# Stages two and three of a five-stage attention and MLP kernel in one written order, with weight units cut into eight steps

## The chip, the cores and the metric

The kernel runs on one core of a Trainium2 chip. The metric is the device time of one execution in microseconds (us). The engines are TensorE (PE, matmuls; PEld is its weight load), VectorE (DVE), ScalarE (ACT), GpSimd (POOL) and SyncE (SP), which here issues nearly all DMAs.

## The reference, cut to what matters

```python
# attention in chunks of 64, 8 batches x 8 heads x 576 tokens, head size 64
scores = matmul(q_c, k_c.T) / 8;  attn = softmax(scores);  x = matmul(attn, v_c)   # 4608 tokens x 512
# first MLP, 512 -> 1536 -> 512
xn = x / sqrt(mean(x * x) + 1e-6) * rms_g
x = (silu(xn @ w_gate) * (xn @ w_val)) @ w_out
# second MLP, 512 -> 2048 -> 512
h = x @ w_in
out = (h * cos(h)) @ w_out2
```

The weights arrive as 64-bit floats. The kernel takes them apart by integer operations into fp32, splits every fp32 operand into a high and a low half, and multiplies with three matmuls for one (high by high, high by low, low by high).

## The kernel before, in words

**Stages.** Stage one is the attention, the norm, and the first four of the twelve 128-wide column blocks of gate and value as plain products. Stage two is the other eight blocks of gate and value, as two-by-two block products in the seven-product scheme of Strassen and Winograd. Stage three is `w_out` of the first MLP, stage four `w_in` of the second, stage five its `w_out`, all in the seven-product scheme. Stages two to five walk the 4608 tokens in six passes of 768 (NB = 6, halves of H = 384). A *product* below is one of the seven for one group of weights: 12 matmuls of 128x128 by 128x384. Stage two has 4 groups and so 28 products a pass, stage three 3 groups and 21, stages four and five 28 each.

**Stage two (L671 to L780).** Per group the products go 1, then 4 and 3 of the group before, then 2, 6, 5, 7. Products 1, 6, 7 and 4 accumulate in one PSUM bank (`b1`, two of them in turn); after 1, 6 and 7 ACT copies the bank away (`savedg`, L713) before the next of them may write it. DVE adds the copies to banks `b2` and `b5` (L720), and ACT (Silu, L725) or DVE (the multiplication with value, L730) ends a block, which SP stores to `hd`. The operands of the next pass (`operandg`: DVE additions, an ACT cast for the high half, a DVE subtraction for the low) are made one after each product of a pass's last group.

**Weight units.** 44 units (`todo_w`) prepare the weights of stages three to five beside the matmuls. A unit is four raw loads of 128 KB, an ACT pass (L116), four DVE conversions (L119 to L125), for the 16 units of kind "in" an ACT scaling (L232), four DVE sums (L192), two ACT casts (L200), two POOL subtractions (L204) and the stores of the seven results to DRAM (`w_keep`, L213). `w_tick` runs a whole unit after every fourth product of stage two; the last 8 units (LATER) run in stage three, two in each of passes 1 to 4. Stage one prepares the 16 units of stage two in the same way, in the steps a, b, c, d, h, o, k of `prep_step`.

**Stage three (L835 to L914).** `operand2` makes operands five products ahead of PE. A group's next pass comes back from DRAM as one 1.5 MB load (`fetch2`, L303), issued once the last operand of that group is made. The third group of the first pass has its own pool, opened where stage two's tiles lay.

**What sets the order.** Stage one stands in a written table (`ORDER`) that fixes all five queues. Stages two and three are written as loops, and the framework's scheduler orders their instructions on each queue; all queues run in order.

Of the kernel before, what the change touches and what calls it, by code (L numbers as in the profile page):

```python
# [38 lines left out]
LATER = 8  # L39
# [31 lines left out]
SECOND = (1, 2, 6, 7, 5, 4, 3)  # L71
# [8 lines left out]
def kernel(  # L80
# [47 lines left out]
    second_w = [("out1", g, PLACE_A[j]) for j in PRODUCTS for g in range(N1 // 4)]  # L128
    wanted += second_w[:3] + [("h", 0, g) for g in range(N1 // 4)]
    wanted += [("op2", g, k) for g in range(2) for k in range(2)] + second_w[3:]  # L130
    wanted += [("prep", 0, k) for k in range(6)]
# [10 lines left out]
    def free(*tags):  # L142
        for tag in tags:
# [6 lines left out]
            if kind in ("h", "x2"):  # L150
                early[key] = wp.tile([P, 2, H], F32, tag=tag, name="a")
                if kind == "h":
                    a = hd[0][:, k, 0:2, :H]
# [12 lines left out]
    raws, least = [], [LATER]  # L166
# [21 lines left out]
    def w_sums(t, s):  # L188
        ops = ((t[:, 3, :], t[:, 2, :], ALU.add), (s[:, 0, :], t[:, 0, :], ALU.subtract))
        ops += ((t[:, 0, :], t[:, 3, :], ALU.subtract), (t[:, 1, :], s[:, 1, :], ALU.subtract))  # L190
        for n, (a, b, op) in enumerate(ops):
            nc.vector.tensor_tensor(s[:, n, :], a, b, op=op)  # L192

    def w_parts(to, t, s):
        to = [to[0][:, :, 0:3], to[0][:, :, 3:7]] if len(to) == 1 else to
        return zip(to, (t[:, :3, :], s))

    def w_hi(to, t, s):
        for o, a in w_parts(to, t, s):
            nc.scalar.copy(o[:, 0], a)  # L200

    def w_lo(to, t, s):
        for o, a in w_parts(to, t, s):
            nc.gpsimd.tensor_tensor(o[:, 1], a, f32(o[:, 0]), op=ALU.subtract)  # L204

    def w_keep(kind, i, half, to):
# [3 lines left out]
        cut = (slice(0, 7),) if len(to) == 1 else (slice(0, 3), slice(3, 7))  # L210
# [4 lines left out]
    def w_load(get):  # L215
        while len(todo_w) > least[0] and len(raws) < 2:
            raw = get("raw", [P, 4, P], U64)
            raws.append((*todo_w.pop(0), raw))
            w_raw(*raws[-1])

    def w_tick(get):
        if not raws:
            return
        kind, i, half, raw = raws.pop(0)
        t = get("pt", [P, 4, P], U32)
        raw, flat = raw.rearrange("p a b -> p (a b)"), t.rearrange("p a b -> p (a b)")
        convert0(raw, flat)
        convert1(flat)
        convert2(raw, flat)
        t = f32(t)  # L230
        if kind == "in":
            nc.scalar.activation(t, t, AF.Copy, scale=-INV2PI)  # L232
        s = get("ps", [P, 4, P], F32)
        w_sums(t, s)
        to = get("pout", [P, 2, 7, P], F32R)
        to = to if isinstance(to, list) else [to]
        w_hi(to, t, s)
        w_lo(to, t, s)
        w_keep(kind, i, half, to)
        w_load(get)  # L240


    def blocks(raw):

        i = (slice(0, 2), slice(2, 4)), (slice(0, H), slice(H, T))
        return {(r, c): raw[:, i[0][r], i[1][c]] for r in range(2) for c in range(2)}
# [45 lines left out]
    def fetch2(s, g):  # L292
        if s < NB:
            t = rw[g].tile([P, 4, T], F32, tag=f"raw{g}", name="rawh")
            raw[s, g] = blocks(t)
            c = s * T % PIECE
            a = hd[s * T // PIECE][:, g, :, c : c + T]
            if ("h", s, g) in early:
                raw[s, g][0, 0] = early["h", s, g]
                nc.sync.dma_start(out=t[:, :, H:], in_=a[:, :, H:])  # L300
                nc.sync.dma_start(out=t[:, 2:, :H], in_=a[:, 2:, :H])
            else:
                nc.sync.dma_start(out=t, in_=a)  # L303
# [11 lines left out]
    def fetchg(s):  # L315
        if s < NB:
            o = s * T % PIECE
            for r in range(2):
                for c in range(2):
                    rawg[s, r, c] = t = gr.tile([P, 2, H], F32, tag=f"r{r}{c}", name="q")  # L320
                    a = xd[s * T // PIECE][:, 2 * r : 2 * r + 2, o + c * H : o + (c + 1) * H]
                    nc.sync.dma_start(out=t, in_=a)

    def operandg(s, j):
        b = {(r, c): rawg[s, r, c] for r in range(2) for c in range(2)}
        if j == 6:
            nc.vector.tensor_tensor(b[0, 0], b[0, 0], b[0, 1], op=ALU.subtract)
            nc.vector.tensor_tensor(b[0, 0], b[1, 1], b[0, 0], op=ALU.add)
        elif j == 7:
            nc.vector.tensor_tensor(b[0, 1], b[1, 1], b[0, 1], op=ALU.subtract)  # L330
        elif j == 5:
            nc.vector.tensor_tensor(b[0, 1], b[1, 1], b[0, 0], op=ALU.subtract)
        elif j == 4:
            nc.vector.tensor_tensor(b[1, 0], b[1, 0], b[0, 0], op=ALU.subtract)
        a = b[{1: (0, 0), 2: (1, 0), 6: (0, 0), 7: (0, 1), 5: (0, 1), 4: (1, 0), 3: (1, 1)}[j]]
# [868 lines left out]
```

## Time and profile before

| | |
|---|---|
| median of 3 runs | 1701.04 us (1699.08 to 1701.77) |
| the profiled execution | 1701.35 us, its span 1699.6 us |
| PE, DVE, ACT, POOL busy | 96%, 82%, 57%, 11% of the span |
| mean granted TensorE clock | 0.99 |
| DMA | 343 MB, 202 GB/s over the span |

Matmuls overlap in the pipeline, so a busy PE is not yet a PE at its pace. What a stage loses is read from its length against that of a stage of the same matmuls that waits for nothing; what it loses it to is read from the waits of PE, and from there back along the queue that PE waited for.

### The profile page before, as it was taken

How to read it: one execution, taken by the hardware profiler on the slowest of the kernel's cores; microseconds unless marked ns; L12 is line 12 of the kernel's file. 1: busy time of each engine (PE TensorE's matmuls, PEld its weight loads, DVE VectorE, ACT ScalarE, POOL GpSimd, SP SyncE). 2: the span in 40 equal slices, each digit the busy share in tenths (PEclk: the TensorE clock that was granted, in tenths of full speed). 3: DMA queues.
4: the chain of work that ended last, by engine and by line, in shares of the span. 5: the costliest groups of instructions: out<-in, count | busy, mean ns of one | idle time of the engine just before them, and what ended most of it. 6: DMA issues, size and time to landing. Idle time of an engine off the chain costs nothing.

```text
span 1699.6 us, 29170 instructions
## 1 busy us (share of the span) xinstructions
PE 1631.2 (96%) x11208; PEld 1566.0 (92%) x11208; DVE 1385.6 (82%) x1926; ACT 965.4 (57%) x1382; POOL 190.2 (11%) x208
## 2 busy tenths in 40 slices
PE   6999999999999999899999999999999999999999
PEld 5887788889889889899999999999999999999998
DVE  7998886578888888489988768889889978878876
ACT  5777665344555554245554458888888744444433
POOL 2322322022232222001110000000000000000000
PEclk9999999999999999989999999999999999999999
DMA  9588897968768788955556874344334673365341
GB/s 341 180 250 271 267 279 241 387 196 266 214 202 253 218 226 241 369 180 184 181 172 234 271 277 140 112 149 140 130 121 142 204 244 111 87 185 145 115 113 38
DMA packets 338956, 342.98 MB, mean 202 GB/s; under 512 B 87680, under 2 KB 303744, under 8 KB 338816
## 3 DMA queue, kind: packets, MB, share of 16 engines
q1 hardware_dynamic: 338016, 341.02, 62.8%
q8 instruction: 88, 1.44, 0.4%
q14 instruction: 52, 0.43, 0.1%
q10 hardware_dynamic: 800, 0.10, 0.0%
HBM read 197.92 MB, written 143.13 MB: 201 GB/s over the span
## 4 chain that ended last, share of the span: by engine, by line
PE 66%; DVE 17%; DMA 7%; ACT 4%; issue 3%; SPq 1%; POOL 1%; DVEq 0%; ACTq 0%; POOLq 0%
PE b L285 56%; PE v L285 4%; PE g L285 4%; DMA rawh<-hd 3%; DMA raw<-in_w_dram 2%; DVE z L720 2%; DVE ps L192 1%; DVE xt L346 1%; DVE pt L125 1%; DVE z L730 1%; DVE pt L124 1%; DMA hd<-z 1%; PE pt L435 1%; ACT xo L272 1%; DVE xo L273 1%
## 5 line engine op out<-in xcount | busy, mean ns | idle before, releaser
L285 PE MATMUL b<-xo,w 128*128 128x384 f32 x3528 | 622.4, 337 | 15.0 <-ACT xo L272 12.6
L285 PEld LDWEIGHTS b<-xo,w 128*128 128x128 f32 x3528 | 615.4, 189 | 21.7 <-ACT xo L272 16.6
L285 PE MATMUL b<-xt,w 128*128 128x384 f32 x1728 | 316.0, 339 | 23.4 <-ACT z L713 18.4
L285 PEld LDWEIGHTS b<-xt,w 128*128 128x128 f32 x1728 | 302.0, 190 | 33.8 <-ACT z L713 25.0
L285 PE MATMUL b<-x,w 128*128 128x384 f32 x1440 | 264.3, 336 | 1.7 <-DVE z L720 1.6
L285 PEld LDWEIGHTS b<-x,w 128*128 128x128 f32 x1440 | 251.1, 188 | 4.8 <-DVE z L720 3.1
L272 ACT CAST xo<-q 128x768 fp32r<-128x768 f32 x144 | 118.2, 836 | 117.3 <-PE b L285 98.5
L273 DVE TENSOR_TENSOR xo<-q,xo 128x768 fp32r<-128x768 f32 x144 | 135.1, 954 | 53.3 <-ACT xo L272 53.0
L285 PE MATMUL b<-q,w 128*128 128x384 f32 x864 | 158.2, 334 | 0.0
L285 PEld LDWEIGHTS b<-q,w 128*128 128x128 f32 x864 | 150.5, 188 | 0.0
L272 ACT CAST xo<-rawh 128x768 fp32r<-128x768 f32 x102 | 81.7, 834 | 96.5 <-DMA rawh<-hd 51.6
L273 DVE TENSOR_TENSOR xo<-rawh,xo 128x768 fp32r<-128x768 f32 x102 | 92.9, 953 | 25.4 <-ACT xo L272 25.1
L285 PE MATMUL g<-xt,w 128*128 128x512 f32 (+1 forms) x528 | 111.4, 363 | 1.7 <-DVE xt L502 1.7
L285 PE MATMUL v<-xt,w 128*128 128x512 f32 (+1 forms) x528 | 108.7, 357 | 0.3 <-ACT sg L548 0.3
L285 PEld LDWEIGHTS g<-xt,w 128*128 128x128 f32 x528 | 88.2, 194 | 15.8 <-DVE xt L502 2.2
L204 POOL TENSOR_TENSOR pout<-pt,pout 128x384 fp32r<-128x384 f32 x44 | 49.5, 1125 | 474.4 <-ACT pout L200 420.3
L285 PEld LDWEIGHTS v<-xt,w 128*128 128x128 f32 x528 | 85.6, 189 | 13.9 <-ACT sg L548 0.5
L720 DVE TENSOR_TENSOR z<-b,z 128x768 f32<-128x768 f32 x72 | 68.3, 950 | 30.4 <-PE b L285 12.8
L998 DVE TENSOR_TENSOR u<-b,z 128x768 f32<-128x768 f32 x72 | 68.6, 952 | 17.7 <-ACT z L993 16.7
L1014 ACT ACTIVATE q<-q 128x768 f32<-128x768 f32 x72 | 60.8, 844 | 34.8 <-DVE q L1013 34.8
L1016 DVE SCALAR_TENSOR_TENSOR q<-q,u 128x768 f32<-128x768 f32 x72 | 68.6, 952 | 12.7 <-ACT q L1015 12.2
L1013 DVE SCALAR_TENSOR_TENSOR q<-q,u 128x768 f32<-128x768 int32 x72 | 68.6, 953 | 12.4 <-ACT q L1012 12.3
(132 smaller groups left out, 2052.0 us busy)
## 6 DMA issues: line engine op xcount, KB each, us to landing
gd<-q SPq DMA_DIRECT2D x80, 384.0 KB, 2.5
q<-gd SPq DMA_DIRECT2D x80, 384.0 KB, 4.2
w<-kout SPq DMA_DIRECT2D x49, 512.0 KB, 7.4
rawh<-hd SPq DMA_DIRECT2D x15, 1536.0 KB, 7.3
raw<-in_w_dram SPq DMA_DIRECT2D x176, 128.0 KB, 3.2
qk<-in_qk_dram SPq DMA_DIRECT2D x36, 512.0 KB, 5.4
kout<-pout SPq DMA_DIRECT2D x40, 448.0 KB, 3.7
kgv<-wout SPq DMA_DIRECT2D x32, 448.0 KB, 5.6
```

Of the source, the lines that this page charges most:

```text
L124: nc.vector.scalar_tensor_tensor(t, hi, 0xC0000000, t, op0=ALU.bitwise_and, op1=ALU.bitwise_or)
L125: nc.vector.scalar_tensor_tensor(t, lo, 29, t, op0=ALU.logical_shift_right, op1=ALU.bitwise_or)
L192: nc.vector.tensor_tensor(s[:, n, :], a, b, op=op)
L204: nc.gpsimd.tensor_tensor(o[:, 1], a, f32(o[:, 0]), op=ALU.subtract)
L272: nc.scalar.copy(hi, a)
L273: nc.vector.tensor_tensor(lo, a, f32(hi), op=ALU.subtract)
L285: nc.tensor.matmul(acc, a, b, start=first and k == 0 and q == 0, stop=k == n - 1 and q == 2, skip_group_check=True)
L720: nc.vector.tensor_tensor(part, acc, part, op=ALU.add)
L998: nc.vector.tensor_tensor(t, acc, part, op=ALU.add)
L1013: nc.vector.scalar_tensor_tensor(q, k, -1.0, u, op0=ALU.mult, op1=ALU.add)
L1014: nc.scalar.activation(q, q, AF.Sin, scale=math.pi)
L1016: nc.vector.scalar_tensor_tensor(q, q, -PI2, u, op0=ALU.add, op1=ALU.mult)
```

## The change

One table, `ORDER2`, now writes out the order of stages two and three for all five queues. Its tokens are single steps: M is a product of stage two, N one of stage three, A, B, C the PSUM copies, a, e, y the sums, ends and stores, q, h, l additions, high and low of an operand of stage two, u, i, o the same of stage three, G the load of one block, P a step of a weight unit, W, F, J, K, L, V the places that come free for a weight or a block that is waiting to be loaded.

- A weight unit has the steps l (loads), a, b, c, s (scaling, kind "in"), d (sums), g and h (casts), o and p (POOL), k and m (stores), each with its own place. The sums are written into the raw tile, the conversion tile has two buffers, the results two tiles of 3 and 4.
- LATER is 10: units 34 to 43 run in stage three, in passes 1 to 5.
- Stage three's rows of hidden values come back as four blocks of 384 KB each, each loaded when that block is free. Six blocks of its first pass are loaded early into places of their own (before: three), among them all four of the third group. Its first products go 1, 1, 2, 2, 7, 7 over the first two groups before the third group is touched (before: 1, 1, then 1 of the third).
- Stage two's products go 1, 4 and 3 of the group before, 6, 2, 7, 5, and its operands follow.
- The kept weights have high and low side by side (`[P, 7, 2, 2, 2, P]` with the high/low index last but one), so a store writes runs of 1024 B where it wrote 512 B; the matmuls index them accordingly.
- In stage one the table `ORDER` is another one as well (995 tokens for 1009). The sums of its 16 units move from DVE to POOL, it starts on the plain products with column block 2 in place of 0, converts the first weight unit later, and leaves 14 of the 28 weight loads of stage two to `ORDER2`.

```diff
-LATER = 8
+LATER = 10
-SECOND = (1, 2, 6, 7, 5, 4, 3)
+SECOND = (1, 6, 2, 7, 5, 4, 3)
...
+    w1st = [(g, j) for j in (1, 2, 7) for g in range(2)] + [(2, 1), (2, 7)] + [(g, 6) for g in range(3)] + [(2, 2)]
+    w1st += [(g, j) for j in (5, 4, 3) for g in range(N1 // 4)]
+    second_w = [("out1", g, PLACE_A[j]) for g, j in w1st]
...
-        for h in range(2):
-            for o, k in zip(to, cut):
-                nc.sync.dma_start(out=kept[kind, g][:, k, e, h, half], in_=f32(o[:, h]))
+        nc.sync.dma_start(out=kept[kind, g][:, k0 : k0 + to.shape[1], e, half], in_=f32(to))
...
+    def w_step(kind, u):
+        key = todo_w[u]
+        late = u >= len(todo_w) - LATER
...
+        s = f32(raw)[:, : 4 * P].rearrange("p (a b) -> p a b", b=P)
+        if kind == "a":
+            convert0(raw, flat)
+        elif kind == "b":
+            convert1(flat)
+        elif kind == "c":
+            convert2(raw, flat)
         elif kind == "s":
             nc.scalar.activation(t, t, AF.Copy, scale=-INV2PI)
+        elif kind == "d":
+            w_sums(t, s, nc.vector)
...
-                nc.sync.dma_start(out=t, in_=a)
+    def fetch2(s, g, b):
+        raw[s, g, b] = t = rw[g].tile([P, 2, H], F32, tag=f"r{g}{b}", name="rawh")
+        r, c = b // 2, b % 2
+        o = s * T % PIECE + c * H
+        nc.sync.dma_start(out=t, in_=hd[s * T // PIECE][:, g, 2 * r : 2 * r + 2, o : o + H])
...
                 b["s"] = pp.tile([P, 4, P], F32, tag="ps", name="wsum")
-                w_sums(t, b["s"])
+                w_sums(t, b["s"], nc.gpsimd)
...
-            if count[0] % 4 == 0:
-                if count[0] == 4:
-                    w_load(getg)
-                elif pg:
-                    w_tick(getg)
...
+    ORDER2 = """
+        Pl0 M001 q06 q07 h06 l06 A00 h07 l07 q05 M002 M006 q04 h03 B00 M007 h05 l05 M005 M011 l03 h04 l04 C00 Pa0 Pb0
...
+    with tc.manual_schedule(engines=FIXED):
+        for name in ORDER2.split():
+            if name[0] == "P":
+                w_step(name[1], int(name[2:]))
```

What this does to the queues, at three places. First ACT, in a late group of a pass of stage two. The names: `z<-b` is the copy of the PSUM bank that PE waits for, `pout` (after: `wout`) the casts of a weight unit, `pt` (after: `wt`) its first pass and its scaling, `xt` and `x` operand casts. Before:

```order
L713 COPY z<-b_6058 128x768
L232 ACTIVATE pt<-pt 128x512
L200 CAST pout<-pt 128x384
L200 CAST pout<-ps 128x512
L116 ACTIVATE pt<-raw 128x512
L232 ACTIVATE pt<-pt 128x512
L200 CAST pout<-pt 128x384
L725 ACTIVATE z<-z 128x768
L200 CAST pout<-ps 128x512
L713 COPY z<-b_6058 128x768
```

After:

```order
L749 COPY z<-b_5706 128x768
L246 CAST wout<-wraw 128x4x128
L235 ACTIVATE wt<-wt 128x512
L349 CAST x_4560<-q 128x768
L349 CAST xt<-q 128x768
L749 COPY z<-b_5706 128x768
L246 CAST wout<-wt 128x3x128
L246 CAST wout<-wraw 128x4x128
L349 CAST xt<-q 128x768
L116 ACTIVATE wt<-wraw 128x512
L749 COPY z<-b_5706 128x768
```

Before, eight instructions of two weight units and one Silu stood between the first and the second copy of a bank; now the steps of a unit are spread, and four stand between two copies.

Second PE, at the start of stage three. `b1`, `b2` and `b3` are the banks of products 1, 2 and 7, each operand is an `xo`, and `xo_8147` (before) and `xo_8184` (after) are the first of the third group. Before, from the last matmul of the second group's product 1:

```order
L285 MATMUL b1_8160<-xo_8092,w_7647 128x384
L285 MATMUL b1_8160<-xo_8147,w_7663 128x384
L285 MATMUL b3_8214<-xo_8152,w_7823 128x384
L285 MATMUL b1_8160<-xo_8147,w_7663 128x384 x11
L285 MATMUL b3_8214<-xo_8152,w_7823 128x384 x11
L285 MATMUL b3_8214<-xo_8157,w_7837 128x384 x12
```

After:

```order
L290 MATMUL b1_8103<-xo_7755,w_7668 128x384
L290 MATMUL b2_8133<-xo_8101,w_7777 128x384 x12
L290 MATMUL b2_8133<-xo_8146,w_7779 128x384 x12
L290 MATMUL b3_8164<-xo_8148,w_7885 128x384 x12
L290 MATMUL b3_8164<-xo_8181,w_7887 128x384 x12
L290 MATMUL b1_8103<-xo_8184,w_7988 128x384 x12
```

Four products of the first two groups now stand ahead of the third group's first.

Third SP, between two passes of stage three. `rawh<-hd` reads hidden values back, `x2d<-x` stores a result, `raw` (after: `wraw`) and `kout` are the loads and stores of weight units. Before:

```order
L186 DMA raw<-in_w_dram 128x4x32 x4
L906 DMA x2d_72<-x_8752 128x2x384
L303 DMA rawh<-hd_70 128x4x768
L906 DMA x2d_72<-x_8806 128x2x384
L303 DMA rawh<-hd_70 128x4x768 x2
L906 DMA x2d_72<-x_8885 128x2x384
L213 DMA kout_8647<-pout 128x3x128
```

After:

```order
L301 DMA rawh<-hd_70 128x2x384 x2
L841 DMA x2d_72<-x_8684 128x2x384
L301 DMA rawh<-hd_70 128x2x384 x2
L201 DMA kout_7837<-wout 128x3x256
L189 DMA wraw<-in_w_dram 128x4x32 x4
L841 DMA x2d_72<-x_8785 128x2x384
L301 DMA rawh<-hd_70 128x2x384 x6
```

Before, three large loads followed the last operands; now twelve small ones are spread over the end of a pass and the start of the next.

## Rows read from the trace of the kernel before

**Rows 1.** Windows by stage, us: length, busy (instructions) per engine, clock, DMA share, GB/s.

```profile
0.00:319.10 319.10, 294.13 (x3648) 248.96 (x3648) 260.00 (x507) 201.50 (x366) 81.82 (x122) 0.98 0.83 269
319.10:707.30 388.20, 363.95 (x2016) 352.56 (x2017) 305.15 (x469) 191.60 (x283) 87.70 (x70) 0.99 0.80 248
707.30:992.90 285.60, 271.53 (x1514) 266.14 (x1514) 239.49 (x291) 131.71 (x174) 20.69 (x16) 0.98 0.66 217
992.90:1343.60 350.70, 350.70 (x2018) 349.05 (x2017) 300.28 (x350) 290.46 (x376) 0.00 (x0) 1.00 0.41 142
1343.60:1699.60 356.00, 350.91 (x2018) 349.27 (x2016) 280.67 (x311) 150.17 (x186) 0.00 (x0) 1.00 0.47 138
```

**Rows 2.** Waits of PE in stage two: us in total, times, longest.

```profile
PE b L285 <- ACT z L713: 18.4, 16, 3.3
PE b L285 <- DVE z L720: 5.3, 9, 1.1
```

**Rows 3.** Timeline around one of them: start, length, engine, [idle before].

```profile
489.82 1.12 DVE L192 TENSOR_TENSOR ps<-pt,ps 128x128 f32<-128x128 f32 x1
490.97 0.62 ACT L200 CAST pout<-ps 128x512 fp32r<-128x512 f32 x1 [0.51 <-DVE ps L192]
491.50 0.79 ACT L713 COPY z<-b 128x768 f32<-128x768 f32 x1
...
492.34 3.88 PE L285 MATMUL b<-xt,w 128*128 128x384 f32 x13 [3.32 <-ACT z L713]
```

**Rows 4.** Windows of 10 us with a lower granted clock, columns as in rows 1.

```profile
720.00:730.00 10.00, 5.46 (x16) 5.06 (x17) 7.83 (x11) 4.77 (x7) 0.00 (x0) 0.53 0.53 124
490.00:500.00 10.00, 7.66 (x36) 7.66 (x37) 6.19 (x12) 5.86 (x10) 2.18 (x3) 0.83 0.73 210
```

**Rows 5.** Groups of DVE in stage two: busy us, mean ns | idle before.

```profile
L720 DVE TENSOR_TENSOR z<-b,z 128x768 f32<-128x768 f32 x71 | 67.4, 950 | 29.2 <-ACT z L713 12.5 <-PE b L285 11.7 <-DMA w<-kout 5.1
...
L119 DVE TENSOR_SCALAR pt<-pt 128x512 f32<-128x512 f32 x35 | 23.7, 676 | 32.3 <-ACT pt L116 32.3
...
L192 DVE TENSOR_TENSOR ps<-pt,ps 128x128 f32<-128x128 f32 x35 | 19.1, 546 | 0.7
...
L120 DVE TENSOR_SCALAR pt<-pt 128x512 uint32<-128x512 uint32 x35 | 14.8, 424 | 0.9
...
L332 DVE TENSOR_TENSOR q<-q 128x768 f32<-128x768 f32 x6 | 9.3, 1546 | 0.1
```

**Rows 6.** Landing of the weight loads of stage two, DMA view: KB each, median us.

```profile
w<-kgv SPq DMA_DIRECT2D x28, 512.0 KB, 8.5
```

**Rows 7.** Waits in stage three, of PE and of ACT.

```profile
PE b L285 <- ACT xo L272: 12.6, 9, 6.5
...
ACT xo L272 <- DMA rawh<-hd: 51.6, 15, 5.6
```

**Rows 8.** Pieces of PE in stage three, timeline.

```profile
724.50 45.17 PE L285 MATMUL b<-xo,w 128*128 128x384 f32 x241 [6.46 <-ACT xo L272]
...
773.16 0.44 PE L285 MATMUL b<-xo,w 128*128 128x384 f32 x1 [0.42 <-ACT xo L272]
...
819.63 0.45 PE L285 MATMUL b<-xo,w 128*128 128x384 f32 x1 [1.51 <-ACT xo L272]
...
915.18 0.44 PE L285 MATMUL b<-xo,w 128*128 128x384 f32 x1 [1.51 <-ACT xo L272]
```

**Rows 9.** Windows of the start of stage one, columns as in rows 1.

```profile
0.00:40.00 40.00, 24.45 (x458) 20.54 (x461) 31.11 (x60) 20.09 (x38) 9.17 (x20) 0.91 0.99 341
40.00:140.00 100.00, 94.84 (x1385) 85.46 (x1378) 94.99 (x189) 74.06 (x138) 29.70 (x42) 1.00 0.72 223
```

**Rows 10.** Groups of stage one's weight units, columns as in rows 5.

```profile
L204 POOL TENSOR_TENSOR wout<-wsum,wout 128x512 fp32r<-128x512 f32 x16 | 22.0, 1374 | 0.0
...
L204 POOL TENSOR_TENSOR wout<-wt,wout 128x384 fp32r<-128x384 f32 x16 | 16.8, 1052 | 44.3 <-ACT wout L200 33.8 <-DVE z L426 6.2 <-DVE wt L120 3.7
...
L192 DVE TENSOR_TENSOR wsum<-wt 128x128 f32<-128x128 f32 x32 | 9.1, 284 | 0.1
```

More of the change, by code (lines that the diff above doesn't have):

```diff
@@ L191, in w_sums, with w_keep @@
         for n, (a, b, op) in enumerate(ops):
[L192 to L206, printed above, removed]
+            eng.tensor_tensor(s[:, n, :], a, b, op=op)
+    def w_keep(kind, i, half, to, k0):
         g, e = i // 2, i % 2
@@ L290, with block2, blocks2 @@
     raw, ops = {}, {}
[L292 to L302, printed above, removed]
-                nc.sync.dma_start(out=t, in_=a)
+    def fetch2(s, g, b):
[3 more added lines that the diff above has]
+        nc.sync.dma_start(out=t, in_=hd[s * T // PIECE][:, g, 2 * r : 2 * r + 2, o : o + H])
+    def block2(s, g, b):
+        return early["h", g, b] if s == 0 and ("h", g, b) in early else raw[s, g, b]
+    def blocks2(s, g):
+        have = [k for k in range(4) if (s, g, k) in raw or (s == 0 and ("h", g, k) in early)]
+        return {k: block2(s, g, k) for k in have}
     xstack = ExitStack()
@@ L781 @@
-    xstack.close()
     third = ExitStack()
@@ new lines, in storeg, with open2, turn2 @@
+    def storeg(s, g, k):
+        r, c = k // 2, k % 2
+        t0 = s * T + c * H
+        o = t0 % PIECE
+        to = hd[t0 // PIECE][:, g // 2 + 1, 2 * r : 2 * r + 2, o : o + H]
+        nc.sync.dma_start(out=to, in_=sums[s, g, k])
+    def open2():
+        first.close()
+        rw[0] = rw[1] = second.enter_context(tc.tile_pool(name="rw", bufs=1, side="right", reuse_waits="tile"))
+    def turn2():
+        mid.close()
+        xstack.close()
+        pool["xo"] = rest.enter_context(tc.tile_pool(name="xo", bufs=7, reuse_waits="tile"))
+        pool["tp"] = rest.enter_context(tc.tile_pool(name="tp2", bufs=1, reuse_waits="tile"))
+        pool["ps"] = rest.enter_context(tc.tile_pool(name="ps_c", bufs=1, space=PSUM, reuse_waits="tile"))
+        rw[2] = second.enter_context(tc.tile_pool(name="rw3", bufs=1, side="right", reuse_waits="tile"))
@@ new lines, in hi2, with lo2 @@
+    def hi2(s, g, j):
+        if ("op2", g, 0) in place_of and s == 0 and j == 1:
+            to = [wp.tile([P, 2, H], F32R, tag=place_of["op2", g, e], name="xo") for e in range(2)]
+        else:
+            o = pool["xo"].tile([P, 2, 2, H], F32R, tag="xo", name="xo")
+            to = o[:, 0], o[:, 1]
+        nc.scalar.copy(to[0], source2(s, g, j))
+        ops[s, g, j] = to
+    def lo2(s, g, j):
+        to = ops[s, g, j]
+        nc.vector.tensor_tensor(to[1], source2(s, g, j), f32(to[0]), op=ALU.subtract)
@@ new lines, in multiply2 @@
+    def multiply2(s, g, j):
+        bank = BANK[j]
+        opens = j in (1, 2, 7, 4)
+        if opens and g == 0:
+            tag = "b2" if bank == "b4" else bank
+            z[s, bank] = pool["ps"].tile([P, 2, D], F32, tag=tag, name=bank, bufs=2 if bank == "b1" else 1)[:, :, :H]
+        w, x = weight["out1", g, PLACE_A[j]], ops.pop((s, g, j))
+        for p in range(2):
+            steps = [(w[:, e, p, 0], w[:, e, p, 1], x[0][:, e], x[1][:, e]) for e in range(2)]
+            mm3(z[s, bank][:, p], steps, opens and g == 0)
@@ L917 @@
+    rest.close()
     G4 = N2 // 4
```

537 lines of the change are left out of this document (265 added, 272 removed).

## The prediction

> **What bounds the kernel now.** I read the windows by stage first, then the waits of PE in the two stages that the table rewrites, then the timeline back from a long wait, then stage one. In the windows by stage [rows 1] stage four is the yardstick: its 2016 matmuls (6 passes, 28 products of 12) take 350.7 us at a granted clock of 1.00 with PE busy throughout, so 0.174 us for a matmul and 2.09 us for a product. Stage two holds the same 2016 matmuls of the same shape and takes 388.2 us: 37.5 us too many. Stage three holds 1512, worth 263.0 us, and takes 285.6: 22.6 too many. Stage five's 356.0 us hold the same matmuls, the end of the output included, and nothing in the change reaches it. So the two rewritten stages can give back 60 us at most, and PE is the bound: DVE is busy for 305.2 us in stage two and 239.5 in stage three, which fits into 350.7 and 263.0.
>
> In stage two PE waits 23.7 us in 25 pieces [rows 2], and 18.4 of them wait for ACT's copy of a PSUM bank. The timeline shows what that is [rows 3]: the copy itself takes 0.8 us, but it stood behind a weight unit's second cast, which waited for the unit's last sum on DVE, and PE stood for 3.32 us. The rest of the 37.5, some 14 us, is what follows such a wait: in the ten microseconds around it the granted clock is 0.83, a mixture of 2.4 and 1.2 GHz [rows 4].
>
> Stage three loses its 22.6 us at two kinds of place [rows 8]. From its start at 707.3 to 773.16 stand 26 products, worth 54.3 us; they took 65.9, so 11.6 are lost, of which 6.46 are the wait for the third group's first operand, and in the window behind it the clock is 0.53 [rows 4]. After that a pass should take 21 products, 43.8 us: 773.16 to 819.63 is 46.5, and the two up to 915.18 take 95.6, so 2.6 and 7.9 are lost. At those borders ACT's casts wait for the 1.5 MB loads, 51.6 us in 15 waits [rows 7], most of it hidden.
>
> **The change part by part.** *Stage two's order.* It removes no PE work. One unit fewer runs here (34 against 35 between the stage's limits), so DVE's load stays near 305 us, or 0.87 of 350.7. The chance lies in the places: between two copies of a bank stand four ACT instructions instead of eight, and the casts that wait for sums no longer come as a block ahead of the copy. The changed sequence 1, 4, 3, 6, 2, 7, 5 gives the copies of product 1, 6 and 7 two, one and two products of time (4.2, 2.1, 4.2 us) where it was three, one and one; a copy of 0.8 us behind one other ACT instruction of the same size fits into each. So nearly all of the 23.7 us of waits can go, and with them the slow clock. What is late next: first, the opening, where product 6 follows 1 and 2 directly and its operand needs two additions, a cast and a subtraction, some 3.5 us against 2.1 (1 to 2 us). Second, 14 of the 28 weight loads now stand in this stage's SP queue, some directly ahead of the product that reads them in the table (fourth group, first pass); a load lands in 8.5 us [rows 6], and SP reaches the first of them only after stores that wait for POOL, so I count 2 us and bound it by 0 and one full landing, 8.5. Third, the table gives the second and the fourth pass about 8% more of DVE's work than the mean, 55 us and more of 58.5; small hold-ups remain there, 3 us. Fourth, 2 us for waits of single semaphores. That leaves 8 to 9 us of the 37.5: **29 us saved**, between 15 (half the waits come back elsewhere) and 35.
>
> *Stage three's blocks.* The third group's four blocks come early into places of their own and four products of the other groups, 8.4 us, stand ahead of it, against a wait of 6.46: the 11.6 us of the start shrink to about 2. The single blocks are loaded as each comes free, most of them during the last two products of a pass instead of after its last operand; that is up to six multiplications, 12.5 us, earlier for the first two of the four. Of the 10.5 us at the borders I leave 3. The cost: 72 loads instead of 18, hidden on SP, which idles between the passes, and two weight units more. Those lie in pass 5, which had none, so each of passes 1 to 5 holds two as passes 1 to 4 did. A unit's eight DVE instructions at 0.3 to 0.7 us [rows 5] are some 3.5 us, so of the 239.5 us [rows 1] the 8 units are 28, a pass without them 35, and with two 42, for 43.8. That is close, so 1 us more. Stage three then loses 6 of its 22.6: **16.6 us saved**, between 5 and 20.
>
> *Stage one.* DVE is busy 126 of the first 140 us [rows 9] and PE's clock and busy share are low in the first 40, so DVE sets the pace there. The 64 sums leave DVE: 64 times 0.284 is 18.2 us. On POOL the trace has no such sum; the two POOL sizes of a unit, 1.374 us for 512 columns and 1.052 for 384, differ by 0.32 for 128 columns and leave a base of 0.09, so I take 0.41 us, 26 us in all beside POOL's 82 of 319. What POOL does slows some of DVE's work: in stage two the last sum of a unit took 0.546 where it takes 0.284, the first conversion 0.676 against 0.424 of its neighbour, and the operand addition of the row 1.546 against 0.95 of a plain sum [rows 5, 10]. Over 35 units that is some 9 us (35 times 0.26) and 9 (35 times 0.25), and for some 20 such additions 12: 30 us over POOL's 87.7 [rows 1], or 0.34 us for one of POOL's. So the 26 us cost DVE 9, and 9 remain as gain, a third of it in the stretch that DVE bounds. The new table also brings the first normed operands up about 4 us of DVE work earlier, by moving the first unit's conversion back. **6 us saved**, between a loss of 8 (the rule below) and a gain of 14.
>
> The Trainium skill speaks against this part: "SBUF — State Buffer", section "SBUF: two separate sides", has GpSimd and a DVE instruction with two SBUF inputs take the shared ports by an exclusive lock, the other blocked for the whole instruction. The rows above show a third of that as a mean. By the rule the 26 us of POOL would cost DVE 26 and the 6 us gained become some 8 lost; that is the second rival.
>
> *The wider runs of the kept weights and the moved raw buffers* are costed at nothing: DMA is at 0.80 of its time in stage two, and no wait in rows 2 and 7 is for a store. If that cover is gone, the weight loads are what comes late, and it is in the first rival. *Stages four and five* keep their time; the loads of the first weights of stage four start about nine products, 19 us, before it, against a landing of 8.5 each and several together, so 0 to 3 us, taken as 0.
>
> Sum: 29 + 16.6 + 6 = 51.6 us. The profiled execution took 1701.35 us (span 1699.6, 1.75 around it), 0.3 above the median. 1701.35 - 51.6 = 1649.8, and I say **1649 us**.
>
> **The rivals.** *First, the waits move to the SP queue.* One strict order for all queues means that a store that waits for POOL holds every load behind it; then weights and blocks arrive late in each pass. Against it: SP's order was fixed before too, and DMA has a fifth of its time free. If half of stage two's waits come back (15 saved) and half of stage three's (11 saved), with nothing from stage one: 1675 us. *Second, POOL's sums lock DVE in full.* Stage one then loses 8 instead of gaining 6, and DVE sets its pace there: 1649 + 14 = 1663. For it, DVE at 126 of 140 us; against it, the third measured in stage two. *Third, slower.* Every unit now crosses between ACT, DVE and POOL at eight written places, and a place that comes too early holds a queue. The longest single wait of PE is now 3.3 us [rows 2]. If each of the 44 units costs PE 2.7 us, that is 119 us against the 60 lost today: 1699.6 + 1.75 + 59 = 1760. It decides from 1.4 us of PE time for each unit on; today it is 60 / 44, the same 1.4, so the table would have to be no better than the scheduler's order. Between the two copies in the order I see the reverse. *Fourth, no difference:* the written order ends up with the scheduler's waits, 1700.
>
> **How the numbers follow.** Forecast 0.73, first rival 0.11, second 0.07, third 0.06, fourth 0.03. For the range I take both ends of the terms, not all at once: 35 + 20 + 11 saved gives 1635; 15 + 11 + 0 gives 1675, the first rival, whose better half is in. So 1634 to 1674, which leaves out the third and fourth, half of the first, and a little of the forecast's own spread. A measurement of this kernel tells some 0.2% (3.4 us) from no change. Faster: 0.73 + 0.11 + 0.07 = 0.91; the same 0.03; slower 0.06.
>
> **What would show it.** In the changed profile stage two should last about 359 us with PE's waits for the PSUM copy under 5 us and the clock at 1.00 in all but one or two windows; stage three about 269, with no wait over 2 us at its start and none for a block; stage one about 313, with POOL's busy time 26 us up and DVE's some 10 us down. A stage two above 370 says that waits moved: if PE waits for a weight load, it is the first rival, if for ACT behind POOL or DVE, the third. A stage one above 319 is the second. The forecast is wrong if stages two and three together stay above 650 us.

## The result, and the profile after

The changed kernel takes **1651.24 us** (median; 1651.09 to 1651.34) against 1701.4 us beside it: a ratio of 0.9707, interval 0.9691 to 0.9724. The prediction was 1649. The profiled execution took 1651.34 us, its span 1649.1. The sum came out, but not all of its terms did.

The windows by stage answer [rows 1]. Columns: window and length, then busy us (instructions) of PE, weight loads, DVE, ACT and POOL, the granted clock, DMA share, GB/s. The third window ends after the first product of stage four; the fourth is a hole that was not there before.

```profile
0.00:311.10 311.10, 288.79 (x3649) 246.46 (x3649) 239.88 (x434) 199.96 (x361) 112.04 (x184) 0.99 0.83 273
311.10:663.80 352.70, 351.46 (x2017) 349.17 (x2018) 303.42 (x461) 187.74 (x280) 90.86 (x68) 1.00 0.80 259
663.80:929.90 266.10, 264.46 (x1525) 263.94 (x1523) 246.28 (x306) 134.87 (x181) 31.04 (x20) 1.00 0.74 244
929.90:942.90 13.00, 0.17 (x2) 0.05 (x1) 1.06 (x2) 3.72 (x5) 0.00 (x0) 0.61 0.86 341
942.90:1293.60 350.70, 350.70 (x2006) 349.09 (x2007) 300.63 (x350) 286.45 (x371) 0.00 (x0) 0.99 0.41 138
1293.60:1649.10 355.50, 350.44 (x2015) 348.81 (x2014) 280.20 (x311) 149.81 (x185) 0.00 (x0) 1.00 0.47 137
```

Stage one is 8.0 us shorter than before, stage two 35.5. Stage three runs from 663.8 to the first matmuls of stage four at 927.78: 264.0 us, 21.6 less and 1.0 above what its matmuls are worth; PE runs through it in two pieces (start, length, engine, line, what, [idle before <- releaser]), so that neither the 11.6 us at its start nor the 10.5 at its borders are lost any more:

```profile
663.76 256.00 PE L290 MATMUL b<-xo,w 128*128 128x384 f32 x1476
921.41 6.53 PE L290 MATMUL b<-xo,w 128*128 128x384 f32 x36 [1.64 <-ACT s L826]
```

Stage four then ends at 1293.6, 365.8 us after its start, where it took 350.7: 15.1 more. Stage five is 0.5 shorter. Together: 8.0 + 35.5 + 21.6 - 15.1 + 0.5 = 50.5, the difference of the spans.

All of PE's waits in stage two, where [rows 2] had 23.7 us (us in total, times, longest):

```profile
PE b L290 <- ACT z L749: 0.9, 1, 0.9
PE b L290 <- DVE h L563: 0.8, 1, 0.8
PE b L290 <- DVE z L753: 0.4, 1, 0.4
```

The new hole stands at the border of stages three and four. The timelines of PE, of DVE and of SP's queue (SPq), columns as above; `w<-kin` loads a weight of stage four, `x2d<-x` stores a result of stage three:

```profile
927.78 2.25 PE L290 MATMUL b<-q,w 128*128 128x384 f32 x12
942.86 6.09 PE L290 MATMUL b<-q,w 128*128 128x384 f32 x24 [12.83 <-DVE x L836]
```

```profile
923.64 0.95 DVE L836 TENSOR_TENSOR x<-b,s 128x768 f32<-128x768 f32 x1
941.84 0.96 DVE L836 TENSOR_TENSOR x<-b,s 128x768 f32<-128x768 f32 x1 [17.25 <-DMA x2d<-x]
942.72 0.95 DVE L715 TENSOR_TENSOR x<-tmp,x 128x768 fp32r<-128x768 f32 x1
```

```profile
915.74 15.24 SPq L163 DMA_DIRECT2D w<-kin  x14
931.93 0.37 SPq L841 DMA_DIRECT2D x2d<-x  x1
933.20 0.32 SPq L163 DMA_DIRECT2D w<-kin  x1
942.83 0.37 SPq L841 DMA_DIRECT2D x2d<-x  x1
```

Read from the bottom. SP spends 15 us on 14 weight loads of 512 KB before it comes to the store of the total of product 5. That store leaves the queue at 931.93 and lands only just before 941.84, since the loads ahead of it still fill the engines (the DMA share is 1.03 from 930 to 940). The next total on DVE goes into the same single tile `x2`; it waits 17.25 us, holds the PSUM bank that PE needs for product 2 of stage four, and holds the lows of stage four's operands (`L715`) behind it.

The Trainium skill ("DMA: Bandwidth & Descriptors", section "Queues, rings and completion order") says that each engine takes a ring's descriptors in the order in which they were put there. This trace agrees: the store took 9.9 us behind the loads, where the median landing of these stores in stage three is 3.3.

### The profile page after: what moved, and what is told of

The parts are those of the page before. It is cut to its first block, busy times and chain, and to the rows that moved or that the text cites. A ratio compares the mean times of both kernels' runs of the same rounds, so it can differ in the third digit from the quotient of the medians.

```text
span 1649.1 us, 29190 instructions
## 1 busy us (share of the span) xinstructions
PE 1606.0 (97%) x11208; PEld 1557.5 (94%) x11208; DVE 1371.5 (83%) x1862; ACT 962.6 (58%) x1382; POOL 233.9 (14%) x272
## 2 busy tenths in 40 slices
DMA packets 293131, 342.98 MB, mean 208 GB/s; under 512 B 87936, under 2 KB 265600, under 8 KB 292992
## 4 chain that ended last, share of the span: by engine, by line
PE 90%; DVE 5%; DMA 2%; issue 1%; ACT 1%; POOL 0%; SPq 0%; DVEq 0%; ACTq 0%; POOLq 0%
PE b L290 78%; PE g L290 4%; PE v L290 4%; PE sc L400 1%; PE o L456 1%; PE tr L489 1%; PE pt L440 1%; DMA w<-kin 1%; DMA x2d<-x 1%; DVE p L433 1%; DVE z L430 1%; DMA kgv<-wout 0%; DMA q<-x2d 0%; DVE xn L481 0%; DVE mx L413 0%
## 5 line engine op out<-in xcount | busy, mean ns | idle before, releaser
L290 PE MATMUL b<-xo,w 128*128 128x384 f32 x3528 | 613.3, 334 | 2.5 <-ACT s L826 1.6
L290 PE MATMUL b<-xt,w 128*128 128x384 f32 x1728 | 304.9, 335 | 1.7 <-ACT z L749 0.9
L248 POOL TENSOR_TENSOR wout<-wt,wout 128x384 fp32r<-128x384 f32 x44 | 52.6, 1196 | 441.1 <-ACT wout L246 390.3
L749 ACT COPY z<-b 128x768 f32<-128x768 f32 x72 | 57.6, 800 | 86.1 <-PE b L290 68.1
L290 PE MATMUL g<-xt,w 128*128 128x512 f32 (+1 forms) x528 | 107.5, 355 | 0.0
L811 DVE TENSOR_TENSOR xo<-rawh,xo 128x768 fp32r<-128x768 f32 x98 | 100.5, 1058 | 5.8 <-ACT xo L806 5.8
L290 PEld LDWEIGHTS g<-xt,w 128*128 128x128 f32 x528 | 85.7, 189 | 13.1
L1032 DVE TENSOR_TENSOR u<-b,z 128x768 f32<-128x768 f32 x72 | 68.4, 951 | 20.1 <-ACT z L1027 16.7
L1047 DVE SCALAR_TENSOR_TENSOR q<-q,u 128x768 f32<-128x768 int32 x72 | 68.5, 952 | 13.2 <-ACT q L1046 13.1
```

The costliest lines, as they stand in the source:

```text
L248: nc.gpsimd.tensor_tensor(b[n][:, :, 1], a, f32(b[n][:, :, 0]), op=ALU.subtract)
L290: nc.tensor.matmul(acc, a, b, start=first and k == 0 and q == 0, stop=k == n - 1 and q == 2, skip_group_check=True)
L749: nc.scalar.copy(sums[s, g, k], z[s, g, "b1"])
L811: nc.vector.tensor_tensor(to[1], source2(s, g, j), f32(to[0]), op=ALU.subtract)
L1032: nc.vector.tensor_tensor(t, acc, part, op=ALU.add)
L1047: nc.vector.scalar_tensor_tensor(q, k, -1.0, u, op0=ALU.mult, op1=ALU.add)
```

## The experiments

Each is one edit to the changed kernel, 1651.24 us; where another kernel is the base, it is said.

**The border: a tile of its own.**

```diff
-        ... tag="s1" if (s, j) == (NB - 1, 3) else "x2", name="x2")
+        ... tag={3: "s1", 4: "s5"}.get(j, "x2") if s == NB - 1 else "x2", name="x2")
```

> The changed kernel with one edit: the last pass's third total of stage three is written into the tile of product 5's sum, which is free by then, and no longer into the single tile from which the total before it is still being stored. Theory: PE's new wait of 12.8 us at the border of stage three to stage four hangs on this tile; the store that must empty it stands on SP behind 14 weight loads of 512 KB, and the total that waits for it holds the PSUM bank that PE needs and the lows of stage four's operands. Then the wait falls under 2 us, the stretch keeps its clock, and the time is 1638 to 1641 us. Rival one, the weight loads themselves are the limit: the same wait comes back as a wait for a weight load, 1647 to 1651 us. Rival two, the lows behind that total are late by themselves: PE waits 4 to 8 us for DVE, 1643 to 1647 us.

**The border: the stores ahead of the last loads, besides.** The end of the table (J: a load; d, t: DVE; w: a store):

```diff
-        N504 N514 N524 c55 N503 N513 N523 t53 J04 J14 J24 J03 d5 t55 w55 t54 w54 J13 w53 J23
+        N504 N514 N524 c55 d5 t55 w55 t54 w54 N503 N513 N523 t53 w53 J04 J14 J24 J03 J13 J23
```

> As the kernel with the tile of its own, and besides the last pass's totals and their three stores stand ahead of the last six weight loads in the table instead of among them. If the tile was the whole cause, this adds nothing: within 2 us of that kernel. If stores that stand behind loads also hold places in memory that stage four's first tiles need, it gains another 1 to 3 us. If the total of product 5, now earlier, waits for the store of the total ahead of it on DVE, it loses 1 to 4 us against it.

Measured: 1642.79 us with the tile alone, **1637.75 us** (1636.64 to 1638.03; ratio to before 0.9623, interval 0.9606 to 0.9640) with both. PE at the border of the one, and then of the other:

```profile
927.77 6.40 PE L290 MATMUL b<-q,w 128*128 128x384 f32 x36
```

```profile
927.03 6.40 PE L290 MATMUL b<-q,w 128*128 128x384 f32 x36
```

Both missed what I had expected: the tile alone takes 1.8 us more than 1641, and the stores gain 5.0 us more, where I had allowed 3 at most. The hole is gone in both, and in the first with the 14 loads where they stood: it was the wait for the one tile, not the loads as such. That the tile alone misses its 1638 to 1641 has another place. Stage four is in no table; a scheduler orders it, and in the two kernels its order on ACT is not the same. With the tile alone ACT's queue goes from 940.49 to the next copy, which PE releases only at 948.8, and the casts of stage four's results stand behind it; PE waits for them later, once, in the row below. With the stores moved the same casts come at 940.45:

```profile
940.49 0.80 ACT L1027 COPY z<-b 128x768 f32<-128x768 f32 x1 [1.32 <-PE b L290]
948.81 0.80 ACT L1027 COPY z<-b 128x768 f32<-128x768 f32 x1 [7.52 <-PE b L290]
```

```profile
956.77 3.40 PE L290 MATMUL b<-q,w 128*128 128x384 f32 x12 [3.87 <-DVE q L1056]
```

```profile
939.75 0.80 ACT L1029 COPY z<-b 128x768 f32<-128x768 f32 x1 [1.32 <-PE b L290]
940.45 1.57 ACT L1048 CAST q<-u 128x768 int32<-128x768 f32 x2
```

Stage four takes 356.5 us in the one and 351.8 in the other. So the 5.0 us between the two kernels are mostly that order, as far as the traces show; what the earlier stores are worth by themselves these runs don't tell.

**Stage two: all steps of a unit in one place; those on ACT and DVE alone; the casts alone.** Three depths of one edit, for stage two's 34 units (of unit 4 the casts' edit is shown):

```diff
-        ... Pd4 f13 q16 M023 a021 Ph3 ... Pk3 Pl5 Pg4 Pa5 Pb5 h17 ... M101 Pm3 Ph4 ...
+        ... Pd4 Pg4 Ph4 f13 q16 M023 a021 ... Pk3 Pl5 Pa5 Pb5 h17 ... M101 Pm3 ...
```

> The changed kernel with the steps of each of stage two's 34 weight units put back into one place of the table (where the sums stood), its raw loads left where they are; the order of products, the rest of the table and stage three are untouched. Theory: the spread of the steps is what took the waits out of stage two, since a cast that waits for DVE's sums no longer stands ahead of the copy of a bank. Then PE waits 15 to 24 us for the copies again, the clock dips behind them, and stage two goes from 352.7 to 370 to 380 us, the whole to 1668 to 1679 us. Rival: the new sequence of products, with more room for the copies of 1, 6 and 7, carries the gain: stage two stays under 358 us, the whole under 1657 us.

> The changed kernel with a unit's steps on ACT and DVE (first activation, conversions, sums, the two casts) in one place of the table, where the sums stand, for the 34 units of stage two; the lows on POOL, the stores and the loads stay where they were. All steps in one place took 8.1 us more for a unit, the casts alone 1.0 us. If the rest is ACT standing through DVE's conversions too (four instructions, some 2.2 us, and four sums, some 1.2 us, between its first activation and its last cast), a unit costs 3 to 5 us of PE: 1755 to 1820 us. If it is SP standing with loads and stores behind the stores that wait for POOL, this kernel stays within 20 us of the one with the casts moved: 1675 to 1706 us.

> The changed kernel in which only the two casts of each of stage two's 34 weight units move: to the place right behind the unit's sums; conversions, lows, stores and loads stay. With all steps of a unit in one place the kernel took 1927 us, 8.1 us more for a unit; this run asks which of the handovers costs. Theory of the prediction (a copy of a bank stands behind a cast that waits for the last sum): ACT is held 1 to 2 us for a unit, and about half of these hit a copy: 10 to 30 us longer, 1661 to 1681 us. Rival: ACT is busy for half of the stage and has room for it, and the cost of the clump lies in the conversions or in the stores behind POOL: under 4 us, 1649 to 1655 us.

| what stands in one place | time, us | more for a unit |
|---|---|---|
| nothing (the changed kernel) | 1651.24 | |
| sums and casts | 1685.71 | 1.0 |
| first activation, conversions, sums, casts | 1777.49 | 3.7 |
| all of a unit, lows and stores too | 1927.34 | 8.1 |

The run without the lows and stores lies within its 1755 to 1820 us; the casts' run lies 4.7 us above the upper end that I had given, the run with all steps 248. The casts alone bring the length of the stage before back. Stage two of that kernel, PE's waits in it, and one of them in the timeline:

```profile
311.60:701.00 389.40, 362.76 (x2017) 356.09 (x2018) 305.53 (x461) 188.58 (x280) 84.57 (x68) 0.98 0.73 236
```

```profile
PE b L290 <- ACT z L749: 22.4, 13, 5.7
```

```profile
351.44 0.28 DVE L195 TENSOR_TENSOR wraw<-wt,wraw 128x128 f32<-128x128 f32 x1
...
352.91 0.52 SPq L201 DMA_DIRECT2D kout<-wout  x1
354.07 0.62 ACT L246 CAST wout<-wraw 128x512 fp32r<-128x512 f32 x1 [4.35 <-DMA kout<-wout]
354.59 0.79 ACT L749 COPY z<-b 128x768 f32<-128x768 f32 x1
...
355.44 1.97 PE L290 MATMUL b<-xt,w 128*128 128x384 f32 x5 [5.65 <-ACT z L749]
```

389.4 us against 388.2 in [rows 1], 22.4 us of waits for the copy against 18.4 in [rows 2], and again PE waits for a copy that stands behind a unit's cast, as in [rows 3]. But the row at 354.07 shows a second reason beside the sums: the cast also waits for its result tile, of which there is one, until the unit before has been stored; and that store stood behind weight loads on SP. Over this stage the casts wait 50.3 us for sums and conversions on DVE and 21.2 for such stores, in the changed kernel 8.4 and 5.0.

With the lows and the stores in that place too, 149.9 us more are lost than without them, and the longest waits are on SP. ACT's and SP's waits of that kernel in stage two:

```profile
ACT z L749 <- DMA hd<-z: 68.9, 11, 10.8
```

```profile
SPq L201 <- POOL wout L248: 419.7, 68, 18.7
```

SP stands 419.7 us with a store that waits for POOL. Behind it stand the stores of the stage's results, and ACT's copies wait 68.9 us for the tiles that these stores would empty. With the lows and stores at their own places SP's same wait is 182.3 us, in the changed kernel 104.0.

**Stage two: the sequence of products.** In 17 of the 24 groups the old sequence, and then again in 11 (in the first of the two, products 6 and 7 of some fourth groups read operands that already belong to the next pass, and four totals of product 2 come after the bank's next use, so that it computes something else):

```diff
-        ... M116 M112 a110 y031 Pk6 Pg7 B11 M117 M115 Pm6 ...
+        ... M112 M116 a110 y031 Pk6 Pg7 B11 M115 M117 C11 Pm6 ...
```

> The changed kernel with the sequence of products in 17 of stage two's 24 groups as before: 1, 4, 3, 2, 6, 5, 7 in place of 1, 4, 3, 6, 2, 7, 5 (the first group of each pass and one more keep theirs, since their operands come in that order); copies and totals keep their places or move as far behind their product as they must. If the new sequence is needed, as the prediction had it (the copy of product 7 now has one product of time, where it had two), PE waits at one copy in three groups of four, 0.3 to 1 us each with the clock behind it: 6 to 20 us longer. If the places of the steps are what matters, under 3 us: 1649 to 1654 us.

> The sequence of products as before (1, 4, 3, 2, 6, 5, 7) again, now only in 11 groups of the second and third weights of a pass, where no operand of the next pass is written between the moved products, and with the total of product 2 of the group before kept ahead of the next product 2. In the run with 17 groups PE's waits were mostly for operands and totals of moved products, which says nothing on the copies. If the new sequence is needed (the copy of product 7 has one product of time, where it had two; a total of product 2 has one product less), the 11 groups cost 0.5 to 1.5 us each, PE's waits for copies and totals and the clock behind them: 5 to 16 us longer, 1656 to 1667 us. If the places of a unit's steps are what matters and the sequence does not, under 3 us: 1650 to 1654 us.

1711.22 us for the first, of which nothing follows: much of its waiting is for the operands and totals just named. 1677.07 us for the second, 25.8 us more, 2.3 for a group, and PE's waits in stage two, beside 0.9 us for the first operand, are these:

```profile
PE b L290 <- ACT z L749: 8.5, 7, 2.3
PE b L290 <- DVE z L753: 7.4, 5, 4.7
PE b L290 <- ACT sg L759: 3.2, 2, 1.6
```

That is above what I had expected of a needed sequence. It shows that the sequence can't be put back alone, as the casts can't: the places of the steps and the sequence of the products fit each other. It doesn't show that a table written for the old sequence would be slower; that was not tried.

**Stage one: the sums back on DVE; the old table with the sums on POOL.**

```diff
-                w_sums(t, b["s"], nc.gpsimd)
+                w_sums(t, b["s"], nc.vector)
```

```diff
-        ORDER = """ Q0 Q1 s0 m0 I Q2 Q3 V0 m1 b0 s1 b1 e0 e1 n0 ...
+        ORDER = """ I Q0 Q1 s0 D00 Q2 V0 Q3 m0 V1 s1 m1 b0 k00 p00 Pl0 ...
```

> The changed kernel with the 64 sums of stage one's weight units back on DVE, at the same places of the table. Theory of the prediction: POOL's sums cost DVE about a third of their own time, so with them back DVE's busy time in stage one rises by 9 to 18 us, POOL's falls by 26 to 30, and stage one takes 3 to 8 us longer, 1654 to 1659 us. Rival, POOL's instructions block DVE in full: DVE's busy time falls or stays and stage one is shorter by up to 8 us, 1643 to 1651 us. Rival, DVE is not what paces the stage under the new table: within 1 us of 1651.

> The changed kernel with stage one in the order of the kernel before (its frees of weight places behind the stage left out, which the second table does), the sums on POOL as in the changed kernel. With the sums back on DVE the new table's stage one took 321.0 us, against 319.1 of the old. If table and sums are independent, the old table with POOL's sums takes 307 to 310 us, the whole 1647 to 1651. If the new table is what makes room for POOL's sums, stage one takes 314 to 319 us, the whole 1654 to 1659. The prediction's split, 3 us of the 6 from the sums and 3 from the table, would give 314 us and 1654.

1660.77 us, 1.8 above the range of the first, and 1656.30, as expected if the new table is what makes room for POOL's sums. Stage one of the two, columns as in the windows above:

```profile
0.00:320.98 320.98, 294.61 (x3648) 250.63 (x3648) 256.92 (x498) 200.59 (x361) 80.80 (x120) 0.99 0.81 264
```

```profile
0.00:316.20 316.20, 291.33 (x3648) 246.84 (x3648) 241.48 (x434) 199.36 (x361) 110.54 (x184) 0.99 0.82 270
```

| stage one, us | sums on DVE | sums on POOL |
|---|---|---|
| old table | 319.1 | 316.2 |
| new table | 321.0 | 311.1 |

The move of the sums is worth 2.9 us under the old table and 9.9 under the new one; the new table costs 1.9 us without the move and gains 5.1 with it. The gain belongs to the pair. In which stretch of the stage it is made, these runs don't tell.

DVE is busy 17.0 us less with the sums on POOL, and POOL 31.2 us more. The sums themselves, by groups of DVE with them there, and of POOL in the changed kernel:

```profile
L195 DVE TENSOR_TENSOR wsum<-wt 128x128 f32<-128x128 f32 x32 | 11.3, 352 | 0.3
...
L195 DVE TENSOR_TENSOR wsum<-wsum,wt 128x128 f32<-128x128 f32 x16 | 5.5, 341 | 0.6
L195 DVE TENSOR_TENSOR wsum<-wt,wsum 128x128 f32<-128x128 f32 x16 | 5.4, 335 | 0.0
```

```profile
L195 POOL TENSOR_TENSOR wsum<-wt 128x128 f32<-128x128 f32 x32 | 16.0, 500 | 33.0 <-DVE wt L125 32.8
...
L195 POOL TENSOR_TENSOR wsum<-wt,wsum 128x128 f32<-128x128 f32 x16 | 8.5, 531 | 0.0
L195 POOL TENSOR_TENSOR wsum<-wsum,wt 128x128 f32<-128x128 f32 x16 | 7.8, 490 | 1.3
```

They took DVE 22.2 us, so the rest of DVE became 5.2 us slower through 31.2 us of POOL: 0.17 us for one of POOL's.

**Stage one: more to POOL.** On the kernel with the stores first, the clamp of the 16 units:

```diff
-                convert1(flat)
+                nc.gpsimd.tensor_scalar(f32(flat), f32(flat), HI_MIN, HI_MAX, op0=ALU.max, op1=ALU.min)
+                nc.vector.tensor_scalar(flat, flat, 3, 0x3FFFFFF8, op0=ALU.logical_shift_left, op1=ALU.bitwise_and)
```

> The kernel with the stores first, 1637.8 us, and besides the clamp of stage one's 16 weight units (one instruction of 128x512 each, 0.4 to 0.5 us on DVE) on POOL. POOL's 64 sums cost DVE almost nothing: its busy time fell by 17.0 us of the 18.2 that they took, and stage one became 9.9 us shorter. If DVE's load sets the pace of stage one, the 7 us that leave it now make the stage 2 to 5 us shorter: 1633 to 1636 us. If the chain through a unit counts, a clamp that takes 1.4 us on POOL and stands behind other work there comes later, the conversion behind it holds DVE, and it is 2 to 15 us longer: 1640 to 1653 us.

1653.47 us, 15.7 more than its base and half a microsecond above the range of the second case. The clamp on POOL, and what DVE waited for it in stage one:

```profile
L586 POOL TENSOR_SCALAR wt<-wt 128x512 f32<-128x512 f32 x16 | 31.9, 1998 | 26.8 <-ACT wt L116 23.4 <-DVE mx L413 2.7
```

```profile
DVE wt L587 <- POOL wt L586: 18.9, 10, 2.8
```

It takes 2.0 us where DVE needs 0.49, and DVE's next instruction waits for it on the spot: DVE gets less work and a wait for it. The sums could move, as I read it, because the instruction that follows them, the cast, is on ACT and has a place some way behind; the clamp has its reader directly behind it on the queue it left. But the clamp also takes four times DVE's time on POOL, a sum one and a half times (0.505 against 0.347 us), and these runs don't separate the two.

**The runs of 512 B.**

```diff
-        nc.sync.dma_start(out=kept[kind, g][:, k0 : k0 + to.shape[1], e, half], in_=f32(to))
+        for h in range(2):
+            nc.sync.dma_start(out=kept[kind, g][:, k0 : k0 + to.shape[1], e, h, half], in_=f32(to[:, :, h]))
```

> The changed kernel with the kept weights again in runs of 512 B: the high and the low halves lie apart, each half is stored by a transfer of its own, and the matmuls read the weights in that layout. Theory: the wider runs gain nothing, since no wait of PE is for a store or a weight load: within 2 us of the changed kernel, 1649 to 1653 us. Rival: the transfers of stage one, where DMA is busy for 0.83 of the time, and at the borders become later, and it costs 4 to 10 us.

1651.14 us (1650.49 to 1653.82), with 348557 packets where the changed kernel has 293131: no difference.

**The blocks of a group together.** The same for passes 2 to 5 and all groups:

```diff
-        ... G101 o025 u024 G100 G120 ... G103 o101 ...
+        ... o003 G100 G101 G103 G102 ...
```

> The changed kernel with the four blocks of a group of stage three read back together for passes 2 to 5, right behind the last operand that the group makes in the pass before, as the kernel before had it; four transfers in a row instead of one. Theory: the operands of the next pass follow a few microseconds behind a landing of some 5 us, so ACT's casts wait for the blocks and PE at the borders of the passes: 8 to 14 us longer, 1659 to 1665 us. Rival: ACT and DVE run far enough ahead, and stage three's gain came from the start alone: under 3 us, 1649 to 1654 us.

1668.36 us, 17.1 more, above my 8 to 14. Stage three takes 281.4 us, where it was 285.6 before and 264.0 in the changed kernel. ACT's waits for blocks in it, and the longest stop of PE with what stood on ACT ahead of it:

```profile
ACT xo L806 <- DMA rawh<-hd: 31.2, 10, 5.2
```

```profile
841.32 0.84 ACT L806 CAST xo<-rawh 128x768 fp32r<-128x768 f32 x1 [4.27 <-DMA rawh<-hd]
845.65 0.83 ACT L806 CAST xo<-rawh 128x768 fp32r<-128x768 f32 x1 [3.50 <-DMA rawh<-hd]
846.39 0.79 ACT L826 COPY s<-b 128x768 f32<-128x768 f32 x1
```

```profile
847.24 90.28 PE L290 MATMUL b<-xo,w 128*128 128x384 f32 x504 [4.87 <-ACT s L826]
```

It is stage two's picture again: two casts wait for their data, the copy of a bank stands behind them, and PE waits for the copy. Of PE's 12.3 us of waits in the stage 6.5 are of this kind; 3.0 are for a weight load and 2.8 for lows.

## Why the prediction was right, and where it was not

| term | foretold, us | measured, us |
|---|---|---|
| stage two | 29 saved (15 to 35) | 35.5 saved |
| stage three | 16.6 saved (5 to 20) | 21.6 saved |
| stage one | 6 saved (-8 to 14) | 8.0 saved |
| stages four and five | 0 (0 to 3 lost) | 14.6 lost |
| sum | 51.6 | 50.5 |

So 1649 was close because two errors cancelled: three gains were 13.5 us too small together, and one loss of 14.6 stood at nothing.

*Stage two: the mechanism was right, the size was off.* The term that failed is the 8 to 9 us left over; the stage lost 2.0. The opening was meant to lose 1 to 2 us and lost 0.85 and 0.89, which are all but 0.4 of the waits above, but not for its reason: the operand of product 6 was in time. The 0.85 are a wait for the first operand of the stage (`h`), the 0.89 for the copy after product 6, which product 7 follows directly there. The late weight loads (2), the dense passes (3) and most of the single waits (2) didn't come. The gain passed the upper end, 35, by half a microsecond. That the place of the casts counts is shown by the casts' run: with the casts alone back at the sums the stage takes 389.4 us, as long as before.

What held the copies was read too narrowly. The prediction named a cast that waits for sums; the result tile that must first be stored is a second reason. And in the wait of [rows 3] itself the cast waited only 0.51 us. Ahead of it on ACT a unit's scaling had waited 4.52 us for a conversion on DVE, so that the scaling, two casts and a Silu all stood directly ahead of the copy:

```profile
488.35 0.63 ACT L232 ACTIVATE pt<-pt 128x512 f32<-128x512 f32 x1 [4.52 <-DVE pt L125]
```

In the kernel before, ten of the sixteen waits for a copy, 13.1 of the 18.4 us, follow a cast or a scaling of a unit on ACT; five, 4.4 us, follow a Silu that waited for a total on DVE. The new table spreads the Silus too: ACT's waits for those totals fell from 37.8 to 2.2 us. No run puts the Silus back alone; in the casts' run they wait 0.4 us, and the stage is long all the same. The part on the sequence of products (two, one and two products of time) isn't shown: the run with the old sequence tells only that table and sequence belong together.

*Stage three: right, and the size was off.* Of the 6 us left over 1.0 came; PE's only wait there is 1.6 us for a copy near its end. The start gave back its 11.6 us where 9.6 were counted, the borders 10.5 where 7.5 were. The blocks' run shows that this table needs the blocks one by one; its 17.1 us are more than the borders had lost before, so they are not the size of that term. The early third group was not undone by itself: that it is what freed the start is argued from the place of the wait.

*The border to stage four: the step that failed.* "The loads of the first weights of stage four start about nine products, 19 us, before it ... so 0 to 3 us, taken as 0." The loads were in fact on time: no wait of PE there is for a weight. I asked whether the moved loads arrive, and not what is queued behind them. On SP that was a store, behind the store a single tile, behind the tile a total on DVE, behind the total a PSUM bank and the next stage's lows. Of the 15.1 us, 12.83 are the wait and the rest what follows it: PE had stood, and the granted clock (third from the end) is 0.67, between its two levels, 1.2 and 2.4 GHz:

```profile
940.00:950.00 10.00, 7.14 (x32) 7.15 (x32) 5.38 (x6) 1.02 (x2) 0.00 (x0) 0.67 0.72 245
```

The two runs at the border give 13.5 us back.

*Stage one: right in size by luck of the split.* A third of the sums' gain and an earlier first operand were to make 6 us. Measured, the sums are worth 9.9 us under this table and the table alone costs 1.9. A sum on POOL took 0.505 us (32.3 / 64) and not the 0.41 taken, so POOL rose by 30.2 against 26; what it took from the rest of DVE was half of what I had estimated, 0.17 us for one of POOL's against 0.34, and DVE fell by 20.1 against some 10. Of these, 17.0 come with the sums, as the sums' run shows; the other 3.1 go with nine instructions that the new table no longer has in this window.

By the Trainium skill's rule ("SBUF — State Buffer", section "SBUF: two separate sides"), taken as the prediction took it, the 31.2 us would have cost DVE all of them, and the second rival would have come. The measurement decides against the full price here: 5.2 us. It does not contradict a lock as such, since these runs don't show how much of POOL's time met a DVE instruction of the kind that the page names.

*The wider runs* were costed at nothing and are worth nothing.

*The rivals.* The first, waits on SP, came true in its mechanism at one place, the border, and there by a store and not by a weight. In stage two the stores of the kept weights do hold SP longer for POOL, 104.0 us where it was 35.6 before, but none of PE's waits there is for a load. The second did not come. The third had the right cause: a unit whose steps come too early costs 1.0 to 8.1 us of the kernel's time, and its price of 2.7 lies between; this table avoids it. The fourth is out.

## What to carry to other kernels

In a strict order an instruction costs whatever stands behind it: ask of each one that can wait (a cast, a store, a total into a single tile) what the queue holds next, and give a copy that frees a PSUM bank a clear queue ahead. When loads are moved forward on a DMA queue, look for the stores that now stand behind them and for the tiles that those stores empty; a tile of its own and stores ahead of the loads gave 13.5 us for an edit of a few lines, though some 5 of them came mostly with another order in stage four. Before you move work to a slower engine, ask how long it takes there and how soon its reader comes: the sums, whose reader had slack, gained, and the clamp, whose reader is the next instruction of the relieved engine, lost.

## What was not expected of the hardware

At the border the DMA engines were busy all the time, at some 400 GB/s (windows of 10 us of the changed kernel, the last two columns), and a store of 384 KB took 9.9 us, where the median of these stores in stage three is 3.3:

```profile
920.00:930.00 10.00, 8.59 (x48) 8.30 (x48) 4.59 (x6) 2.16 (x3) 0.00 (x0) 1.00 1.03 415
930.00:940.00 10.00, 0.02 (x1) 0.00 (x0) 0.00 (x0) 3.72 (x5) 0.00 (x0) 0.64 1.03 408
```

The clamp on POOL (a maximum and a minimum in one instruction) took 2.0 us for 128x512 with one input, more than a subtraction of two inputs of that size there (1.36 us, L599 in stage one of the changed kernel).
